# A top-k attention with a GELU layer behind it, on one core: the weights' words leave x's tile, the first loads go over three queues, and TensorE multiplies zeros until the first k

## The chip, the cores and the metric

The kernel runs on one core of a Trainium2 chip. The metric is the device time in microseconds. Before the change it is 1690.68 us (median of 3 runs, 1690.24 to 1690.7); the profiled execution spans 1690.0 us. In what follows PE is TensorE, DVE VectorE, ACT ScalarE, POOL GpSimd and SP SyncE, which here only issues DMAs.

## The reference

Attention over 8 batches, 8 heads, 576 rows and head size 64, in which each row keeps only its 32 largest scores; the heads are then joined to rows of 512, and these go through a layer of width 2048 with the exact GELU.

```
scores = scale * np.matmul(q, k.transpose(0, 1, 3, 2))
kth = np.partition(scores, -top_k, axis=-1)[..., -top_k:-top_k + 1]
scores = np.where(scores >= kth, scores, -1000000000.0)
attn = softmax(scores)                 # with 1e-9 added to the sum
attn_out = np.matmul(attn, v)
x = attn_out.transpose(0, 2, 1, 3).reshape(4608, 512)
h = x @ w_in                           # 512 x 2048
g = 0.5 * h * (1.0 + erf(h / sqrt(2)))
return g @ w_out                       # 2048 x 512
```

q, k, v and the output are float32. The two weights come as float64 numbers, so the kernel must make float32 of them itself.

## The kernel before

**Slots.** Two heads of a batch are a pair. The work is a list of items: one item is a pair and a tile of 128 rows (or, for the last 64 rows of each head, two pairs together). One turn of the main loop (line 616) is a slot, and slot n works on several items at once, in the order in which the loop writes the instructions. That order is final: each engine takes its instructions in it. In slot n, `scores(n + 2)` makes scores on PE (L291, L295) and copies them on ACT (L299, L300); `top_k(n)` finds the 32 largest of each row on DVE, with four rounds of eight maxima (L342) and three rounds that strike these out (L345); `softmax(n - 1, e)` runs on ACT (L381, L382) for the two heads; `add_small`, `threshold` and `normalise` run on POOL (L374, L357, L393); `inverse(n - 1)` is DVE's reciprocal (L368), written behind the top-k of slot n; `transposes(n - 2)` turns the attention on PE (L410 for the last columns, called the tails, then L428 for each head) and copies it on ACT (L411, L435); `attend(n - 3)` multiplies by v on PE (L459) and copies the result into xT on ACT (L464). Transposes, products by v and the small score product share two PSUM buffers ("tp").

**The layer.** Its products are cut into pieces (L507 for x times w_in, L543 for g times w_out). `mlp(1)` writes one piece, at most 7 or 8 in a slot, if the tokens that the piece needs are ready (`ready`). They become ready when all heads of a tile have been attended, in slot 10 for the first time. What is left over is written behind the last slot.

**xT.** The tile xT holds x transposed: 4 parts of 128 rows with 1152 columns, a ring over two batches.

**Weights.** The weights are cut into 16 units of 256 x 512 numbers. Unit `ORDER[i]` is finished in slot `FIRST + i`, so in slots 1 to 16. `load_weights(n + 2)`, at the end of slot n, fetches the words of a unit. The words go to a buffer that is free at that time: to rows of `w_out_sb` that have no weights yet, to an extra tile "words" of which there is one (units with i = 12 and 15), and, for i = 14 alone, to the columns from `RING - WS` = 640 on of xT, which no token needs yet. Two ACT passes make the exponents at the end of the slot before (L183, L184), a third pass makes the mantissa on ACT (L188) or, from slot `START` = 10 on, on POOL (L199), POOL adds the two (L202), and DVE puts the sign in (L210) at the end of the unit's slot.

**The start.** Ahead of the loop, lines 590 to 603 load k and q of the first two pairs, the words of the first two weight units, transpose q and k of both pairs on PE (L250, four blocks, two blocks, four blocks, each group copied by ACT or DVE in L254), and make the scores of items 0 and 1. A load of a pair is four transfers: for each head 128 KB (L94) and the last 64 rows, 16 KB, called the tail (L97). k of pair 0 goes over ACT's queue, the weights over POOL's, all else over SP's. Before its first issue POOL writes the zeros and the identity that later steps need.

**In slot 10** the loop has a case of its own (line 625): when tokens have just been attended and the next piece waits for them, the tails' transpose is written ahead of the softmaxes, so that pieces can start early.

Of the kernel before, what the change touches and what calls it, by code (L numbers as in the profile page):

```python
# [14 lines left out]
def kernel(  # L15
# [19 lines left out]
    nc = tc.nc  # L35
    f32, i32, u32 = mybir.dt.float32, mybir.dt.int32, mybir.dt.uint32
    bf16, i16, u16 = mybir.dt.bfloat16, mybir.dt.int16, mybir.dt.uint16
# [3 lines left out]
    B, H, S, D = q.shape  # L41
    P = 128
    DM = H * D
# [3 lines left out]
    NM = S // P  # L47
    SM = NM * P
    TL = S - SM
    NJ = NM + 1  # L50
    KO = DM // P
    FT = DFF // P


    RING = 2 * S
# [6 lines left out]
    ps = ctx.enter_context(tc.tile_pool(name="ps", bufs=2, space=bass.MemoryType.PSUM))  # L62
# [4 lines left out]
    w_out_sb = const.tile([P, FT, DM], f32, name="w_out_sb")  # L67
    xT = const.tile([P, KO, RING], f32, name="xT")


    raws = {n: [const.tile([P, NJ, 2, D], f32, name=f"raw_{n}{i}") for i in range(m)]
            for n, m in (("k", 2), ("q", 2), ("v", NP + 1))}
    for ts in raws.values():
        for t in ts[:2]:
            nc.gpsimd.memset(t[:, NM], 0.0)
    make_identity(nc, ident)
    for t in raws["v"][2:]:
        nc.gpsimd.memset(t[:, NM], 0.0)


# [3 lines left out]
    def raw_of(n, pair):  # L84
        return raws[n][pair % len(raws[n])]

    def load(n, pair, queue=None):
        if pair >= n_pairs:
            return
        queue = queue or nc.sync  # L90
        b, h0 = pair // NP, 2 * (pair % NP)
        t, src = raw_of(n, pair), sources[n]
        for e in range(2):
            queue.dma_start(  # L94
                out=t[:, 0:NM, e, :], in_=src[b, h0 + e, 0:SM].rearrange("(t p) d -> p t d", p=P)
            )
            queue.dma_start(out=t[e * TL : (e + 1) * TL, NM, e, :], in_=src[b, h0 + e, SM:S])  # L97

# [3 lines left out]
    WS = 512  # L104
    NWI = KO // 2 * (DFF // WS)
    UNITS = NWI + FT // 2
# [3 lines left out]
    def weights_of(u):  # L110

        if u < NWI:
            c, r = u // 2 * WS, u % 2 * 2
            return w_in, r, c, w_in_sb[:, r : r + 2, c : c + WS]
        r = 2 * (u - NWI)
        return w_out, r, 0, w_out_sb[:, r : r + 2, :]


    ORDER = [0, 1, 2, 3, 8, 9, 4, 5, 10, 11, 6, 7, 12, 13, 14, 15]
    FIRST = 1  # L120
    START = 2 * NP + 2
    words = {}
    low = const.tile([P, 1], f32, name="low")
    nc.gpsimd.memset(low, -EXP0 * 2.0**19)

    def unit_in(n):
        return ORDER[n - FIRST] if 0 <= n - FIRST < UNITS else None

    def load_weights(n, queue=None):

        queue = queue or nc.sync
        u = unit_in(n)
        if u is None:
            return
        src, r, c, dst = weights_of(u)
        if src.dtype == f32:
            for x in range(2):
                queue.dma_start(
                    out=dst[:, x], in_=src[(r + x) * P : (r + x + 1) * P, c : c + WS]
                )  # L140
            return


        half, i = src.bitcast(u16), n - FIRST
        if i != 14:
            if i not in (12, 15):
                at = FT // 2 + 4 * (i % 2)
                t = w_out_sb[:, at : at + 4, :].rearrange("p (a b) n -> p a (b n)", a=2)
            else:
                t = stage.tile([P, 2, 2 * WS], f32, tag="words", name="words")  # L150
            for a in range(2):
                queue.dma_start(
                    out=t[:, a].bitcast(u16)[:, 0 : 4 * WS - 1],
                    in_=half[(r + a) * P : (r + a + 1) * P, 4 * c + 1 : 4 * (c + WS)],
                )
        else:

            assert r + 2 < FT
            t = xT[:, :, RING - WS :]
            for a in range(2):  # L160
                queue.dma_start(
                    out=t[:, 2 * a : 2 * a + 2].bitcast(u16),
                    in_=bass.AP(
                        tensor=half.tensor, offset=half.offset + (r + a) * P * 4 * DM + 1,
                        ap=[[4 * DM, P], [2 * WS, 2], [1, 2 * WS]],
                    ),
                )
        words[u] = t

    def parts(u):  # L170

        t, dst = words[u], weights_of(u)[3]
        if t.shape[1] == 4:
            dst = dst.rearrange("p r (b n) -> p (r b) n", b=2)
        return t[:, :, 0::2], t.bitcast(u16)[:, :, 2::4], dst

    def weights_size(u):
# [11 lines left out]

    def on_pool(u):  # L190

        return ORDER.index(u) + FIRST >= START

    def weights_add(u):
        if u in words:
            w, _, dst = parts(u)
            d = dst.bitcast(i32)
            if on_pool(u):
                nc.gpsimd.tensor_scalar(  # L199
                    w.bitcast(i32), w.bitcast(u32), 2.0**-13, None, op0=ALU.mult  # L200
                )
            nc.gpsimd.tensor_tensor(d, d, w.bitcast(i32), op=ALU.add)  # L202
# [149 lines left out]
    def threshold(i):  # L352

        if i < 0 or i >= N:
            return
        st = stat_of[i]
        nc.gpsimd.tensor_scalar(  # L357
            st["neg"], st["top"][:, :, 0 :: TOPK - 1], -1.0, None, op0=ALU.mult
        )
        nc.gpsimd.tensor_tensor(  # L360
            st["bias"], st["neg"][:, :, 0], st["neg"][:, :, 1], op=ALU.subtract
        )

    def inverse(i):
        if i < 0 or i >= N:
            return
        st = stat_of[i]
        nc.vector.reciprocal(st["rden"], st["den"])  # L368

    def add_small(i):  # L370
        if i < 0 or i >= N:
            return
        st = stat_of[i]
        nc.gpsimd.tensor_scalar(st["den"], st["den"], 1e-9, None, op0=ALU.add)  # L374

    def softmax(i, e):

        if i < 0 or i >= N:
            return
        st, s = stat_of[i], row(i, e)  # L380
        nc.scalar.activation(s, s, func=AF.Prelu, bias=st["neg"][:, e, 1:2], scale=1.0, alpha=STEEP)  # L381
        nc.scalar.activation(  # L382
            s, s, func=AF.Exp, bias=st["bias"][:, e : e + 1], scale=1.0,
            accum_out=st["den"][:, e : e + 1],
        )

    def normalise(i):
        if i < 0 or i >= N:
            return
        st = stat_of[i]  # L390
        for e in range(2):
            s = row(i, e)
            nc.gpsimd.tensor_scalar(s, s, st["rden"][:, e : e + 1], None, op0=ALU.mult)  # L393
# [162 lines left out]
    pieces = []  # L556
# [18 lines left out]
    done = [0]  # L575

    def mlp(n):
        for _ in range(n):
            if done[0] >= len(pieces) or pieces[done[0]][0] > ready[0] or left[0] == 0:
                return  # L580
            pieces[done[0]][1]()
            done[0] += 1
            left[0] -= 1


    ready, left = [0], [0]
    staging = ExitStack()
    stage = staging.enter_context(tc.tile_pool(name="stage", bufs=1))

    load("k", 0, nc.scalar)  # L590
    load("q", 0)
    load("q", 1)
    load("k", 1)
    for n in range(2):
        load_weights(FIRST + n, nc.gpsimd)
    for pair in range(2):
        for piece in transpose_qk(pair, pair == 0):
            piece()
# [12 lines left out]
    for pair in range(2, n_pairs):  # L611
        b, p = divmod(pair, NP)
# [3 lines left out]
    for n in range(ahead):  # L616

        left[0] = 7 if START < n < START + 2 * NP else 8
        weights_add(unit_in(n))
        scores(n + 2)  # L620
        product = attend(n - 3)
        late = n > START + 1
        mlp(1)
        tr = transposes(n - 2)
        if product and done[0] < len(pieces) and pieces[done[0]][0] > ready[0]:

            for piece in tr[:1]:
                piece()
            tr, ready[0] = tr[1:], n_tok[0]
        softmax(n - 1, 0)  # L630
        mlp(1)
        if not late:
            softmax(n - 1, 1)
        mlp(1)
        for piece in tr[:-1]:
            piece()
            ready[0] = n_tok[0]
            mlp(1)
        ready[0] = n_tok[0]
        if late:  # L640
            softmax(n - 1, 1)
        add_small(n - 1)
        for piece in tr[-1:] + prep_in.pop(n, []):
            piece()
            mlp(1)
        mlp(left[0])
        if n < N:
            top_k(n, {3: lambda: inverse(n - 1)})
        else:
            inverse(n - 1)  # L650
        threshold(n)
        normalise(n - 1)

        weights_sign(unit_in(n))
        weights_size(unit_in(n + 1))
        if n >= FIRST:
            load_weights(n + 2)
        if n <= NP:
            load("v", n)
# [36 lines left out]
```

## Time and profile before

| | busy us of 1690.0 | instructions |
|---|---|---|
| PE | 1611.4 | 8480 |
| DVE | 1428.8 | 3042 |
| ACT | 1188.1 | 2147 |
| POOL | 662.5 | 764 |

The page has the span in 40 slices of 42 us, with the busy share of each engine in tenths, and groups of instructions by line, each with its count, busy time, mean length and the idle time ahead of it. Three places matter to this change: the first 15 us, in which the engines wait for the first loads; slot 14, from 169.5 to 189.1 us on PE; and slots 10 and 17, in which the order of the work is touched. A releaser, written behind an arrow, is what ended a wait.

### The profile page before, as it was taken

The numbers are of one execution on the slowest core, as the hardware profiler recorded it, in microseconds if no ns is written. First come the engines' busy times: TensorE is split into PE (matmuls) and PEld (weight loads), VectorE is DVE, ScalarE is ACT, GpSimd is POOL, SyncE is SP. The second block draws the span as 40 slices with busy tenths as digits, with TensorE's granted clock in tenths as the row PEclk, the third lists the DMA queues.
The fourth block names the chain that finished last, engine by engine and source line by source line (L and its number), as shares of the span: only waits on it lengthen the run. The fifth ranks groups of instructions, "written<-read, shape, count | busy, mean of one in ns | idle before, by whom it ended". The sixth has DMA issues, their size and how long they took to land.

```text
span 1690.0 us, 24403 instructions
## 1 busy us (share of the span) xinstructions
PE 1611.4 (95%) x8480; PEld 1093.3 (65%) x8480; DVE 1428.8 (85%) x3042; ACT 1188.1 (70%) x2147; POOL 662.5 (39%) x764
## 2 busy tenths in 40 slices
PE   5659899999999999999999999999999999999999
PEld 3336567676666667676666667676666666766665
DVE  6999798998889888998889888898889988899900
ACT  5778677777777777777777777777777777777730
POOL 3668743333333332333333333333333333333410
PEclk8669999999999999999999999999999999999999
DMA  6422210001100011002110111001110000000000
GB/s 158 135 91 98 78 48 9 11 18 35 29 27 15 27 29 41 1 13 49 25 31 1 35 36 41 1 14 28 32 46 1 27 15 15 21 1 13 7 13 13
DMA packets 126715, 56.10 MB, mean 33 GB/s; under 512 B 117888, under 2 KB 117888, under 8 KB 126592
## 3 DMA queue, kind: packets, MB, share of 16 engines
q1 hardware_dynamic: 125056, 52.16, 11.6%
q0 software_dynamic: 320, 2.10, 0.4%
q8 instruction: 67, 1.10, 0.3%
q14 instruction: 56, 0.46, 0.1%
q10 hardware_dynamic: 1216, 0.30, 0.1%
HBM read 45.08 MB, written 9.44 MB: 32 GB/s over the span
## 4 chain that ended last, share of the span: by engine, by line
PE 87%; ACT 5%; DVE 5%; POOL 1%; issue 1%; DMA 1%; SPq 0%; ACTq 0%; POOLq 0%
PE h_ps L507 29%; PE y_ps L543 28%; PE o L459 8%; PE s_ps L295 7%; PE tp L428 7%; DVE top L342 2%; PE o L469 2%; DVE rest L345 2%; PE tp_qk L250 2%; PE t_ps L291 2%; ACT s L382 1%; PE tp_t L410 1%; PE s_ps L316 1%; ACT s L381 1%; ACT L518 1%
## 5 line engine op out<-in xcount | busy, mean ns | idle before, releaser
L342 DVE MAX8 top<-rest 128x8 f32<-128x576 f32 x864 | 610.8, 750 | 0.0
L507 PE MATMUL h_ps<-xT,w_in_sb 128*128 128x256 f32 (+1 forms) x2560 | 554.7, 362 | 6.8 <-DMA xT<-in_moe_w_out_dram 4.9
L543 PE MATMUL y_ps<-w_out_sb,g 128*128 128x512 f32 x1152 | 549.1, 599 | 0.0
L393 POOL TENSOR_SCALAR s<-s,rden 128x576 f32<-128x576 f32 x288 | 493.5, 1723 | 0.8 <-issue 0.4
L507 PEld LDWEIGHTS h_ps<-xT,w_in_sb 128*128 128x128 f32 x2560 | 430.1, 191 | 69.4 <-issue 18.4
L345 DVE MATCH_REPLACE8 rest<-top,rest 128x576 f32<-128x576 f32 x576 | 424.3, 746 | 0.0
L374 POOL TENSOR_SCALAR den<-den 128x2 f32<-128x2 f32 x144 | 32.0, 222 | 868.7 <-ACT s L382 868.2
L543 PEld LDWEIGHTS y_ps<-w_out_sb,g 128*128 128x128 f32 x1152 | 195.4, 191 | 166.0 <-issue 164.6
L299 ACT ACTIVATE s<-s_ps 128x1024 f32<-128x1024 f32 x128 | 131.5, 1027 | 173.2 <-PE s_ps L295 153.0
L382 ACT ACTIVATE s<-s,bias 128x576 f32<-128x576 f32 x288 | 223.3, 776 | 13.2 <-ACT s L381 0.4
L381 ACT ACTIVATE s<-s,neg 128x576 f32<-128x576 f32 x288 | 223.7, 777 | 0.7 <-POOL neg L357 0.2
L435 ACT COPY pt<-tp 128x512 f32<-128x512 f32 x256 | 146.8, 575 | 98.2 <-PE tp L428 97.6
L345 DVE MATCH_REPLACE8 rest<-top,s 128x576 f32<-128x576 f32 x288 | 212.1, 746 | 0.0
L342 DVE MAX8 top<-s 128x8 f32<-128x576 f32 x288 | 202.2, 745 | 5.1 <-ACT s L300 5.1
L428 PEld LDWEIGHTS tp<-ident,s 128*128 128x128 f32 x1152 | 145.9, 144 | 93.3 <-issue 58.1
L428 PE MATMUL tp<-ident,s 128*128 128x128 f32 x1152 | 177.7, 278 | 6.4 <-ACT pt L411 6.4
L368 DVE RECIPROCAL rden<-den 128x2 f32<-128x2 f32 x144 | 23.6, 164 | 169.8 <-POOL den L374 169.5
L295 PE MATMUL s_ps<-qk 64*128 64x256 f32 x1024 | 156.5, 427 | 0.4 <-ACT s L299 0.4
L459 PE MATMUL o<-pt,raw_v 128*64 128x256 f32 x1280 | 155.1, 389 | 1.8 <-ACT pt L435 1.8
L459 PEld LDWEIGHTS o<-pt,raw_v 128*64 128x64 f32 x1280 | 87.5, 139 | 69.5 <-issue 15.1
L295 PEld LDWEIGHTS s_ps<-qk 64*128 64x128 f32 x1024 | 94.1, 198 | 24.3 <-issue 2.5
L518 ACT ACTIVATE g<-h_ps 128x512 f32<-128x512 f32 x144 | 78.7, 595 | 38.8 <-PE h_ps L507 38.0
(65 smaller groups left out, 1106.7 us busy)
## 6 DMA issues: line engine op xcount, KB each, us to landing
raw_q<-in_q_dram SPq DMA_DIRECT2D x64, 128.0 KB, 2.4
raw_v<-in_v_dram SPq DMA_DIRECT2D x64, 128.0 KB, 2.4
out_dram<-y SPq DMA_DIRECT2D x32, 256.0 KB, 2.2
raw_k<-in_k_dram SPq DMA_DIRECT2D x62, 128.0 KB, 2.4
w_out_sb<-in_moe_w_in_dram SPq DMA_DIRECT2D x12, 511.8 KB, 4.8
w_out_sb<-in_moe_w_out_dram SPq DMA_DIRECT2D x10, 511.8 KB, 3.9
w_out_sb<-in_moe_w_in_dram POOLq DMA_DIRECT2D x4, 511.8 KB, 7.7
words<-in_moe_w_out_dram SPq DMA_DIRECT2D x4, 511.8 KB, 6.5
```

The costliest lines, as they stand in the source:

```text
L295: nc.tensor.matmul(s_ps[:, e, c * 256 : (c + 1) * 256], lhsT=lhsT[rows, :], rhs=qk[rows, KT + c * 256 : KT + (c + 1) * 256], start=True, s ...
L299: nc.scalar.activation(spread(s, S + TL, SM), s_ps, func=AF.Copy, scale=scale)
L342: nc.vector.max(st["top"][:, e, 8 * r : 8 * r + 8], cur[e])
L345: nc.vector.match_replace(rest[:, e], st["top"][:, e, 8 * r : 8 * r + 8], cur[e], LOWEST)
L381: nc.scalar.activation(s, s, func=AF.Prelu, bias=st["neg"][:, e, 1:2], scale=1.0, alpha=STEEP)
L382: nc.scalar.activation(s, s, func=AF.Exp, bias=st["bias"][:, e : e + 1], scale=1.0, accum_out=st["den"][:, e : e + 1],)
L393: nc.gpsimd.tensor_scalar(s, s, st["rden"][:, e : e + 1], None, op0=ALU.mult)
L428: nc.tensor.transpose(tp[:, j * P : (j + 1) * P], s[:, first + j * P : first + (j + 1) * P], ident)
L435: nc.scalar.copy(out=dst, in_=tp.rearrange("p (j n) -> p j n", j=NM))
L459: nc.tensor.matmul(o[e * D : (e + 1) * D, 0:n], lhsT=vt[:, j, e, :], rhs=pt[:, e * NM + j if j < NM else 2 * NM, :], start=(j == 0), stop= ...
L507: nc.tensor.matmul(h_tile(u)[:, i, :], lhsT=w_in_sb[:, ko, f * P : (f + 1) * P], rhs=xT[:, ko, c0 : c0 + n], start=(ko == 0), stop=(ko == ...
L543: nc.tensor.matmul(y_of[sub], lhsT=g_of[u][:, i, sub * P : (sub + 1) * P], rhs=w_out_sb[:, f, :], start=(f == 0), stop=(f == FT - 1),)
```

## The change

Four edits. The words of unit 14 go to the one extra tile, so none are put into xT; to let that tile serve units i = 12, 14 and 15 in turn, the last unit is finished a slot later (slot 17). The first k goes over ACT's queue with its tails on POOL's, q and k of pair 1 follow on SP in the order k, q, and the words of the first two units are issued on SP behind them. PE is given 16 products of zeros, written ahead of the first transposes, for which the zeros of one v buffer are written by DVE. And the special case of the order holds only behind slot 10 (`n > START`).

```diff
-    for ts in raws.values():
-        for t in ts[:2]:
-            nc.gpsimd.memset(t[:, NM], 0.0)
+    for n, ts in raws.items():
+        for t in ts[: 1 if n == "v" else 2]:
+            (nc.vector if n == "v" else nc.gpsimd).memset(t[:, NM], 0.0)
     make_identity(nc, ident)
-    for t in raws["v"][2:]:
+    for t in raws["v"][1:]:
         nc.gpsimd.memset(t[:, NM], 0.0)
...
-    def load(n, pair, queue=None):
+    def load(n, pair, queue=None, queue2=None):
...
+        queue2 = queue2 or queue
...
-            queue.dma_start(out=t[e * TL : (e + 1) * TL, NM, e, :], in_=src[b, h0 + e, SM:S])
+            queue2.dma_start(out=t[e * TL : (e + 1) * TL, NM, e, :], in_=src[b, h0 + e, SM:S])
...
+    WARM = 16
...
-    def unit_in(n):
-        return ORDER[n - FIRST] if 0 <= n - FIRST < UNITS else None
+    SLOT_OF = {u: FIRST + i + (i == UNITS - 1) for i, u in enumerate(ORDER)}
+    UNIT_IN = {n: u for u, n in SLOT_OF.items()}
+    unit_in = UNIT_IN.get
...
-        half, i = src.bitcast(u16), n - FIRST
-        if i != 14:
-            if i not in (12, 15):
-                at = FT // 2 + 4 * (i % 2)
-                t = w_out_sb[:, at : at + 4, :].rearrange("p (a b) n -> p a (b n)", a=2)
-            else:
-                t = stage.tile([P, 2, 2 * WS], f32, tag="words", name="words")
...
-        else:
-
-            assert r + 2 < FT
-            t = xT[:, :, RING - WS :]
...
+        half, i = src.bitcast(u16), ORDER.index(u)
+        if i not in (12, 14, 15):
+            at = FT // 2 + 4 * (i % 2)
+            t = w_out_sb[:, at : at + 4, :].rearrange("p (a b) n -> p a (b n)", a=2)
+        else:
+            t = stage.tile([P, 2, 2 * WS], f32, tag="words", name="words")
...
     def on_pool(u):
 
-        return ORDER.index(u) + FIRST >= START
+        return SLOT_OF[u] >= START
...
-    load("k", 0, nc.scalar)
+    load("k", 0, nc.scalar, nc.gpsimd)
     load("q", 0)
+    load("k", 1)
     load("q", 1)
-    load("k", 1)
     for n in range(2):
-        load_weights(FIRST + n, nc.gpsimd)
+        load_weights(FIRST + n)
+
+
+    idle = raws["v"][0][:, NM].rearrange("p e d -> p (e d)")
+    warm = ps.tile([P, 512], f32, tag="l1", name="warm")
+    for _ in range(WARM):
+        nc.tensor.matmul(warm[:, 0:P], lhsT=idle, rhs=idle, start=True, stop=True)
...
-        if product and done[0] < len(pieces) and pieces[done[0]][0] > ready[0]:
+        if product and n > START and done[0] < len(pieces) and pieces[done[0]][0] > ready[0]:
```

More of the change, by code (lines that the diff above doesn't have):

```diff
@@ L141, in load_weights @@
             return
-        half, i = src.bitcast(u16), n - FIRST
-        if i != 14:
-            if i not in (12, 15):
-                at = FT // 2 + 4 * (i % 2)
-                t = w_out_sb[:, at : at + 4, :].rearrange("p (a b) n -> p a (b n)", a=2)
-            else:
-                t = stage.tile([P, 2, 2 * WS], f32, tag="words", name="words")
[L151 to L155, printed above, removed]
-        else:
-            assert r + 2 < FT
-            t = xT[:, :, RING - WS :]
[L160 to L167, printed above, removed]
+        half, i = src.bitcast(u16), ORDER.index(u)
+        if i not in (12, 14, 15):
+            at = FT // 2 + 4 * (i % 2)
+            t = w_out_sb[:, at : at + 4, :].rearrange("p (a b) n -> p a (b n)", a=2)
+        else:
+            t = stage.tile([P, 2, 2 * WS], f32, tag="words", name="words")
+        for a in range(2):
+            queue.dma_start(
+                out=t[:, a].bitcast(u16)[:, 0 : 4 * WS - 1],
+                in_=half[(r + a) * P : (r + a + 1) * P, 4 * c + 1 : 4 * (c + WS)],
+            )
         words[u] = t
@@ L172, in parts @@
         t, dst = words[u], weights_of(u)[3]
-        if t.shape[1] == 4:
-            dst = dst.rearrange("p r (b n) -> p (r b) n", b=2)
         return t[:, :, 0::2], t.bitcast(u16)[:, :, 2::4], dst
```

## The prediction

> **What bounds the kernel now.** I read the page first, then a table of busy time by stage, then the chain that ended last, then the timeline of each engine around the two places that the chain pointed to.
>
> The busy rows of the page give three regimes: a start in which no engine is full, a stretch in which VectorE (DVE) is full, and from slice 6 on a full TensorE (PE). The table by stage (columns: length, then busy us and instructions of PE, weight loads, DVE, ACT, POOL; clock; DMA share; GB/s) puts numbers on it (the first fence is the page's row of DVE in 40 slices, the second the table):
>
> ```profile
> DVE  6999798998889888998889888898889988899900
> ```
>
> ```profile
> 59.00:70.00 11.00, 5.19 (x29) 3.06 (x25) 11.00 (x23) 8.46 (x14) 7.54 (x7) 0.78 0.43 130
> ...
> 160.00:184.00 24.00, 17.38 (x87) 11.32 (x86) 19.69 (x41) 15.06 (x25) 18.00 (x11) 0.87 0.48 156
> ...
> 260.00:300.00 40.00, 40.00 (x213) 27.72 (x210) 36.34 (x79) 28.88 (x54) 14.28 (x17) 1.00 0.00 1
> ```
>
> From 15 to 135 us DVE has no gap to speak of, from about 228 us PE has next to none; what lies between is neither. So a microsecond won before 228 us is a microsecond of the end, provided nothing on the way takes it back, and one won later than that must come out of PE's own work, which the change leaves as it is.
>
> The chain shows the start. Read it as "start, length, what":
>
> ```profile
> 2.77 6.13 DMA raw_k<-in_k_dram
> ...
> 9.03 1.31 PE tp_qk L250 x5
> 10.37 0.59 ACT qk L254
> 11.01 0.80 PE t_ps L291 x2
> 11.80 2.03 PE s_ps L295 x8
> 13.86 1.02 ACT s L299
> ...
> 15.09 1.41 DVE top L342 x2
> ```
>
> The last 16 KB of the first k take 6.13 us to land; all else waits for them, and DVE begins at 15.09. In the timeline of PE, the second place:
>
> ```profile
> 173.24 0.70 PE L507 MATMUL h_ps<-xT,w_in_sb 128*128 128x256 f32 x2
> 178.84 4.63 PE L507 MATMUL h_ps<-xT,w_in_sb 128*128 128x256 f32 x10 [4.91 <-DMA xT<-in_moe_w_out_dram]
> 183.27 0.42 PE L410 MATMUL tp_t<-ident,s 128*128 128x128 f32 x1
> ```
>
> PE sits for 4.91 us until the words of a weight unit, put into xT by L161, have landed, although these products read xT's columns 0 to 255 and the words lie from column 640 on. ACT waits 4.54 us for the same transfer. Then PE runs slow: ten products in 4.63 us, where twelve of the same shape take 2.86 us at 137 us.
>
> **What the Trainium skill says.** *TensorE: Matmul & The Clock Gate*, Part 1 (the HAM clock gate): PE starts at half clock and gets the full one only after a busy window of about 3.4 us; the window runs freely. The trace agrees and is stricter: after 178.84 the full pace comes only near 184.6, 5.8 us later, that is after one whole window without a gap. At the start PE is still at half pace at 24.4 us. *DMA: Bandwidth & Descriptors*, Queues, rings and completion order: each DMA engine takes turns between the queues, a packet at a time. The trace agrees: between 6 and 8 us the queue with the 4 KB packets of weights had 86.0% of the share and the SP queue with its 256-byte packets 4.6%. Same page, Anatomy of one DMA (the gpsimd path): about 2.0 us fixed for a DMA that GpSimd issues; the trace has its first such packets about 1.4 us after the issue at 2.84.
>
> **The change, part by part.**
>
> *1. First loads.* k's big transfers keep ACT's queue, its tails go to POOL's, the weights go behind q and k on SP. 576 KB of k0 and q0 at the 220 GB/s of 2 to 4 us, from 1.9 us, end at 4.5. k's two big transfers were issued at 0.73 and 1.87 and will be issued at 0.73 and 1.3; they then land near 4.7 (before: 5.2). The tails are issued by POOL after its memsets, which ended at 2.88 and are one shorter, so at 2.7 and 3.3; with 1.4 us to the first packet and about 1 us to finish, the last lands at 5.7; with the page's 2.0 us flat it is 5.3, with the 3.2 us of the quickest weight transfer 6.5. q0's tail (6.9 before, with weights in its way) lands near 5.5. So data are there at 5.7, 3.2 us sooner than 8.9. k1 and q1 are no longer behind weights either. The weights' words land about 15 us; ACT first reads them at the end of slot 0 (24.97 before, about 22 after): hidden.
>
> *2. Products of zeros.* The page has 256 instructions for the 128 t_ps products, so a full product is two instructions, and 16 are 32. Warm, twenty of this shape (L469) take 2.50 us: (2.50-0.27)/19 = 0.117 us each. Cold is not shown in a row long enough: 0.22 from the transposes, up to 0.37 from a pair of t_ps at 11.01 (0.80 less 0.42). I take twice the warm one, 0.235. They start when DVE's memset is done, about 1.1 us. If the clock is released between 4.5 and 7.9 (the first whole window of 3.4 us), they end between 6.6 and 8.3; I take 7.7. So **PE, not the data (5.7), sets the start**: it is in order, and the transposes of k stand behind the zeros. From there all is warm: four transposes of k 0.44; then the chain quoted above, 6.06 us from 9.03 to 15.09, less 0.65 on five transposes, 0.4 on t_ps, 1.0 on s_ps: 4.0. DVE begins at 7.7+0.44+4.0 = 12.1, a gain of **3.0** (2.4 to 4.2; with the slow cold end and a late release, 9.5+4.4 = 13.9, it is 1.2). Without the products it would be 5.9+6.06 = 12.0: they bring next to nothing. DVE is full from then to slot 10, so the whole gain travels.
>
> *3. No words in xT.* In slot 14 (169.5 to 189.1 on PE) I walk the order written in the loop without the wait. ACT: copy of o at 173.3, softmax to 175.3; PE: 12 products to 175.9, tails 176.1, transposes and products to 181.2; ACT's second softmax ends at 179.7 instead of 187.7; DVE, which ends its top-k at 180.1, gets its reciprocal at 180.2 instead of 188.06. PE's next slot begins at 181.2 instead of 189.12. The gain is **7.9**: 4.9 wait, 2.4 slow clock after it, and 0.6 of ACT's copies. The lower end is 7.3, PE's part alone. The words now need the one stage buffer of unit 12; its last reader, DVE's sign of slot 13, is done at 170.6, and SP issues at 173.4 anyway, behind the four loads of q and k. They land by 178 to 180 (4.5 to 6.5 us) and ACT asks for them at 181.5. No new wait, with 1.5 us to spare; SP's next work is a slot later.
>
> *4. Slot 10 in another order.* With `n > START` the tails' copy on ACT stands behind both softmaxes (3.1 us), as in slots up to 9, where the trace shows the price:
>
> ```profile
> 118.89 1.12 PE L428 MATMUL tp<-ident,s 128*128 128x128 f32 x4 [1.88 <-ACT pt L411]
> ...
> 224.16 2.38 PE L459 MATMUL o<-pt,raw_v 128*64 128x256 f32 x20 [1.77 <-ACT pt L435]
> ```
>
> There are two PSUM buffers for these transposes, so the third needs that copy. In slot 10 ACT's softmaxes end at 130.9, the copy at 131.2; PE, which did that group at 130.47 after one more piece of products, would come to it at 129.6 and wait 1.6. The last product then ends 1.5 later, ACT's second gelu (which already waited 0.97 for it) too, and in slots 11 to 13 DVE waits for ACT in each (0.81, 1.97, 0.52), so nothing swallows it: **-1.5** (0 to -1.7).
>
> *5. Unit 15 a slot later.* ACT's two passes (2.3 us) leave slot 16's start, where ACT then waits for PE's o anyway, and enter slot 17's, where ACT had 0.9 us free. The second line above is the place: PE waits there for ACT's copy at 224.1, which comes about 1.25 later. **-1.2** (0 to -1.4). POOL's 5.4 us and DVE's 1.35 move into a slot with room. The memset of raw_v on DVE is hidden, DVE is idle.
>
> The sum: 3.0+7.9-1.5-1.2 = 8.2 us; 1690.7-8.2 = **1682.5**.
>
> **The rivals.** (B) *Parts 4 and 5 are swallowed* by waits on other engines: for it, ACT's order in slot 10 starts the softmax 0.15 earlier; against it, ACT is the releaser in all these waits. 3.0+7.9 = 10.9: 1679.8. (C) *The zeros eat the start*: cold to the end at 0.25 each, PE is free at 9.1 and still slow: 9.1+0.87+6.06 = 16.0, nothing won or 0.9 lost. 7.9-2.7-0.5 = 4.7: 1686.0. For it: 13 us of ragged work did not warm PE before; against: that work had gaps, the zeros have none. (D) *A transfer takes the wait's place*: the words of unit 14 come late behind the loads of q and k and ACT's queue stands instead of PE: 3.0+0-2.7 = 0.3: 1690.4. Against: the 1.5 us of slack. (E) *Slower*: C and D together, 0-0.5-2.7 = -3.2, at worst with 1.6 us more for a colder PE: 1694 to 1695.5.
>
> **Chances.** My forecast 0.60, B 0.18, C 0.14, D 0.05, E 0.03. The range takes in B and C with their spread: 1678 to 1687. Faster by over 0.2% (below 1687.3): 0.60+0.18+0.14 and a little of D's spread: 0.92; the same: 0.05; slower: 0.03.
>
> **What would show it.** The first DVE maximum at about 12.1; 32 more PE instructions, ending near 7.7, the first transpose right behind them; no wait for a DMA in PE's list; slot 14 about 11.5 us instead of 19.6; in slot 10 a PE wait of about 1.6 us for ACT's copy, in slot 17 one of about 3 us. I am wrong if the words' landing or SP's queue appears as a releaser of ACT, if DVE is no longer full from 12 to 130, or if PE past 228 us shows gaps that it did not have.

## The result, and the profile after

The changed kernel takes **1685.08 us** (median of 6 runs, 1683.64 to 1688.61), the kernel before beside it 1690.69 (6 runs, 1689.13 to 1691.72): a ratio of 0.997 with a 95% interval from 0.9957 to 0.9983. It is faster by 5.6 us; the forecast was 1682.5 in a range from 1678 to 1687. The profiled execution of it spans 1682.0 us, that of before 1690.0; the device times of these two are 1683.78 and 1691.79, so they lie 8.0 us apart where the medians lie 5.6 apart. One execution of e3 below took 3166.05 us at a clock of 0.89, where the others had 0.98, and counts in no number here.

The rows of the page for the span in 40 slices, PE of the kernel before, then PE and DVE of the changed kernel:

```profile
PE   5659899999999999999999999999999999999999
...
PE   5559999999999999999999999999999999999999
...
DVE  7998988998889888998989888898889998899900
```

The regimes are the old ones, DVE full first and then PE, but the 8 in slice 5, where PE stood for the words, is gone: PE shows a 9 from slice 4 on. The table by stage (length, then busy us and instructions of PE, weight loads, DVE, ACT, POOL; clock; DMA share; GB/s):

```profile
59.00:70.00 11.00, 3.40 (x19) 2.45 (x20) 11.00 (x25) 10.34 (x19) 7.53 (x7) 0.65 0.48 142
160.00:184.00 24.00, 22.26 (x127) 13.20 (x126) 23.48 (x48) 20.85 (x36) 21.93 (x16) 1.00 0.27 84
260.00:300.00 40.00, 40.00 (x205) 27.99 (x204) 34.82 (x77) 29.58 (x53) 16.21 (x20) 1.00 0.01 1
```

In the second window PE is busy for 22.26 us, where it was for 17.38, and its clock is full. The first and the third window show what did not move: DVE full at 59 to 70, PE full at 260 to 300. (PE's clock is lower in the first, 0.65 instead of 0.78; the ledger below has nothing lost there, since DVE is full.) The chain that ended last, at its start ("start, length, what"):

```profile
1.04 5.40 PE warm L590 x32
6.44 0.45 PE tp_qk L239 x4
...
9.48 1.09 PE s_ps L284 x8
10.59 1.02 ACT s L288
...
11.81 1.41 DVE top L331 x2
```

The products of zeros end at 6.4, the score products run at the full pace (1.09 us for eight, 2.03 before), and DVE begins at 11.81 instead of 15.09. No transfer stands in this chain: PE itself, not the data, sets the start. (The packets of weights that were in the way before are of 8 KB, 256 of 8188 bytes in the trace of before, not of 4 KB as the prediction has it; this changes nothing in its argument.) Slot 14 in the timeline of PE:

```profile
171.23 2.86 PE L496 MATMUL h_ps<-xT,w_in_sb 128*128 128x256 f32 x12
173.93 0.27 PE L399 MATMUL tp_t<-ident,s 128*128 128x128 f32 x1
174.03 1.02 PE L532 MATMUL y_ps<-w_out_sb,g 128*128 128x512 f32 x2
```

Twelve products in 2.86 us without a gap, where before two were followed by 4.91 us of waiting and ten slow ones. The waits of PE from 95 us to the end (line, whom it waited for; us in total, times, longest):

```profile
PE tp_t L399 <- POOL s L382: 11.2, 4, 6.0
PE tp L417 <- ACT pt L400: 3.8, 2, 2.3
...
PE o L448 <- ACT pt L424: 1.8, 1, 1.8
...
PE t_ps L280 <- ACT pt L424: 1.4, 2, 1.2
...
PE tp_t L404 <- POOL s L382: 0.4, 1, 0.4
```

No line of this list names a DMA. What is left are waits for ACT and POOL.

**A ledger by slots.** DVE's reciprocal closes each slot, so its start in two traces tells how much has been won up to there. For slots 10, 12, 14, 16 and 19 it starts at 132.72, 157.59, 188.06, 212.19 and 246.43 us before the change. The gains of the profiled executions against these, in us (the column "start" is the first maximum of DVE against 15.09):

| kernel | start | slot 10 | slot 12 | slot 14 | slot 16 | slot 19 | span |
|---|---|---|---|---|---|---|---|
| after | 3.28 | 3.35 | 2.04 | 9.94 | 10.12 | 7.77 | 8.0 |
| e12, the same again | 2.94 | 3.00 | 1.72 | 9.63 | 9.81 | 7.46 | 7.7 |
| e1, old order of slot 10 | 2.69 | 2.76 | 1.48 | 9.44 | 9.53 | 5.62 | 5.8 |
| e2, no zeros | 2.10 | 2.11 | 2.51 | 10.44 | 10.59 | 6.54 | 6.7 |
| e3, words alone | 1.03 | 1.10 | 0.93 | 8.88 | 9.02 | 5.26 | 4.3 |
| e4, start alone | 2.71 | 2.68 | 1.37 | 1.20 | 1.28 | 1.28 | 1.3 |
| e5, filled waits | 2.15 | 2.26 | 2.32 | 10.27 | 10.43 | 8.09 | 8.3 |
| e6, last unit in slot 18 | 2.08 | 2.12 | 0.52 | 8.48 | 8.62 | 8.61 | 8.8 |
| e7, e6 filled | 2.17 | 2.22 | 2.34 | 10.31 | 10.37 | 10.37 | 10.6 |
| e8, e7 with 8 zeros | 4.00 | 4.03 | 4.42 | 12.36 | 12.52 | 12.52 | 12.7 |
| e10, the same as e8 | 3.30 | 3.34 | 3.73 | 11.67 | 11.83 | 11.81 | 12.0 |
| e9, e7 without zeros | 2.10 | 2.21 | 1.07 | 9.04 | 9.15 | 9.15 | 9.4 |
| e11, before, filled | 1.46 | 1.44 | 1.87 | 2.31 | 2.39 | 2.38 | 2.4 |

Each row is one execution, and so is the row of zeros that they are taken against. That one had a late start: e3 and e11 load and begin as the kernel before does, and their DVE starts at 14.06 and 13.63. Differences along a row hardly depend on this; the column "start" does. The traced executions lie up to 1.7 us off the medians of their kernels (that of e11 1.7 under it, those of e4 and before 1.3 and 1.1 over it), so the ledger tells where time goes, and the medians how much of it there is.

Along the row of after: the words bring 9.94 - 2.04 = 7.90 us; 3.35 - 2.04 = 1.31 are lost between slots 10 and 12, and 10.12 - 7.77 = 2.35 between slots 16 and 19. The experiments ask where these two losses come from, and what the zeros are worth.

### The profile page after: what moved, and what is told of

The parts are those of the page before. It is cut to its first block, busy times and chain, and to the rows that moved or that the text cites. A ratio compares the mean times of both kernels' runs of the same rounds, so it can differ in the third digit from the quotient of the medians.

```text
span 1682.0 us, 24466 instructions
## 1 busy us (share of the span) xinstructions
PE 1608.8 (96%) x8512; PEld 1095.1 (65%) x8512; DVE 1428.6 (85%) x3043; ACT 1189.3 (71%) x2147; POOL 661.9 (39%) x761
## 3 DMA queue, kind: packets, MB, share of 16 engines
HBM read 45.08 MB, written 9.44 MB: 32 GB/s over the span
## 4 chain that ended last, share of the span: by engine, by line
PE 88%; DVE 6%; ACT 4%; issue 1%; POOL 1%; ACTq 0%; POOLq 0%
PE h_ps L496 30%; PE y_ps L532 28%; PE o L448 8%; PE s_ps L284 7%; PE tp L417 7%; DVE top L331 3%; DVE rest L334 3%; PE o L458 2%; PE tp_qk L239 2%; PE t_ps L280 2%; PE tp_t L399 1%; PE s_ps L305 1%; ACT s L371 1%; ACT L507 1%; ACT s L370 1%
## 5 line engine op out<-in xcount | busy, mean ns | idle before, releaser
L284 PE MATMUL s_ps<-qk 64*128 64x256 f32 x1024 | 152.6, 418 | 0.7 <-ACT s L288 0.7
```

The costliest lines, as they stand in the source:

```text
L284: nc.tensor.matmul(s_ps[:, e, c * 256 : (c + 1) * 256], lhsT=lhsT[rows, :], rhs=qk[rows, KT + c * 256 : KT + (c + 1) * 256], start=True, s ...
```

## The experiments

In e1 to e4 the first theory is that of the prediction (the copy on ACT in slot 10 and the two passes of the last unit on ACT take back 1.5 and 1.2 us, the zeros bring next to nothing); the others, and those of the later runs, are named in the expectations. Edits are against the changed kernel, except in e11. e1 to e4 shared one series of the kernel before (median 1690.54), e5 to e8 one (1690.14), e9 to e11 one (1691.01); e12 has its own (1691.06). The ratios are against these.

**e1: slot 10 in the old order.**

```diff
-        if product and n > START and done[0] < len(pieces) and pieces[done[0]][0] > ready[0]:
+        if product and done[0] < len(pieces) and pieces[done[0]][0] > ready[0]:
```

> The changed kernel with the old order in slot 10 put back (the tails' transpose ahead of the softmaxes). Theory on record: the new order costs 1.5 us in slot 10, so this runs 1.5 us below the changed kernel (near 1683.5 against its 1685.1). Rival, from the trace of the changed kernel: PE stands at the tails' transpose for POOL in slot 10 whatever the order, the order costs nothing, and the 1.7 us that were lost between slots 11 and 12 are TensorE's half clock after a wait of 2.3 us; then this runs within 1 us of the changed kernel.

1685.03 us (8 runs), ratio 0.9968 (0.9958 to 0.9979): the time of the changed kernel. From slot 9's reciprocal to slot 11's it takes 22.50 us, the changed kernel 22.56. So the order of slot 10 costs nothing. The tails' transpose in the timeline of PE, first of the changed kernel, then of e1:

```profile
123.54 0.33 PE L399 MATMUL tp_t<-ident,s 128*128 128x128 f32 x1 [1.88 <-POOL s L382]
123.71 1.03 PE L496 MATMUL h_ps<-xT,w_in_sb 128*128 128x256 f32 x4
```

```profile
124.11 0.33 PE L399 MATMUL tp_t<-ident,s 128*128 128x128 f32 x1 [0.62 <-POOL s L382]
124.28 1.89 PE L496 MATMUL h_ps<-xT,w_in_sb 128*128 128x256 f32 x8
```

In either order this transpose waits for POOL's normalised scores, which the prediction did not see (before the change it stood at 127.27 without a wait). When it is through, at 123.5, ACT's softmaxes are nearly done (125.1), the copy follows at 125.22, and the third group, at 125.88, finds its buffer free. The loss between slots 10 and 12 is the same in e1 (2.76 - 1.48 = 1.28), so it is not the order's.

**e2: no products of zeros.**

```diff
-    WARM = 16
+    WARM = 0
```

> The changed kernel without the 16 products of zeros. Theory on record: the data are there at about 5.7 us and the rest of the start runs at half clock, DVE's first maximum comes at 12.0 instead of 11.8, and the time is that of the changed kernel within 0.5 us. Rival: the zeros carry the gain of the start; without them DVE begins at 14 us or later and the time is 2 us or more above the changed kernel.

1685.06 us (5 runs), ratio 0.9966 (0.9954 to 0.9979): no difference in the median. DVE starts at 12.99 instead of the 12.0 worked out; PE at the start:

```profile
5.25 1.09 PE L239 MATMUL tp_qk<-ident,raw_k 128*128 128x128 f32 x4 [5.25 <-DMA raw_k<-in_k_dram]
...
7.12 1.12 PE L239 MATMUL tp_qk<-ident,raw_q 128*128 128x128 f32 x4 [0.36 <-DVE qk L243]
...
9.64 2.08 PE L284 MATMUL s_ps<-qk 64*128 64x256 f32 x8
```

The large blocks of k are there at 5.25 (4.7 was forecast; the tails, forecast at 5.7, have landed when they are needed at 6.34), and all of it then runs at half pace. In this trace nothing is lost between slots 10 and 12 (2.11, 2.51), which is new, but 4.05 us between slots 16 and 19, 1.7 more than in the changed kernel. So the equal medians don't show that the zeros do nothing: in the traces a later start and a larger loss stand against a loss that is absent.

**e3: the words alone.** The start and the order of slot 10 are those of before, there are no zeros; the words of unit 14 in their tile and the last unit a slot later stay.

```diff
...
-    WARM = 16
+    WARM = 0
...
-    load("k", 0, nc.scalar, nc.gpsimd)
+    load("k", 0, nc.scalar)
...
-        load_weights(FIRST + n)
...
+        load_weights(FIRST + n, nc.gpsimd)
...
-        if product and n > START and done[0] < len(pieces) and pieces[done[0]][0] > ready[0]:
+        if product and done[0] < len(pieces) and pieces[done[0]][0] > ready[0]:
```

> The kernel before with one part alone: the words of unit 14 in the extra tile and the last unit in slot 17; start and order of slot 10 as before. Theory: slot 14 shrinks by 7.9 us, slot 17 gives back 1.2: 6.7 us below the kernel before (1684.0). Rival: the words' wait was hidden by DVE or ACT and a wait of another kind takes its place: less than 3 us.

1687.91 us (19 runs), ratio 0.9984 (0.9978 to 0.9991). Slot 14 brings 8.88 - 0.93 = 7.95 us, as forecast, and slots 16 to 19 take 9.02 - 5.26 = 3.76 back, three times the forecast. About 1 us more is lost at the very end: PE's last product ends 5.31 us sooner than before the change (1680.89 against 1686.20), but from there to the end of the span, in which ACT's last copy and the last transfers of the output remain, it takes 4.8 us instead of 3.8.

**e4: the start alone.** The start with its zeros stays; words and order are those of before.

```diff
-    SLOT_OF = {u: FIRST + i + (i == UNITS - 1) for i, u in enumerate(ORDER)}
+    def unit_in(n):
+        return ORDER[n - FIRST] if 0 <= n - FIRST < UNITS else None
...
+            t = xT[:, :, RING - WS :]
...
-        if product and n > START and done[0] < len(pieces) and pieces[done[0]][0] > ready[0]:
+        if product and done[0] < len(pieces) and pieces[done[0]][0] > ready[0]:
```

> The kernel before with the other part alone: first loads over three queues, weights behind them, zeros on PE; the words still go into xT and the order of slot 10 is the old one. Theory: DVE begins 3.3 us sooner and all of it reaches the end: 1687.4. Rival: the gain of the start is swallowed by the free-running clock window further on (slots 9 to 18): anything from 0 to 5 us with a spread between runs of 2 us or more, where the kernel before spreads over 1 to 2.6 us.

1689.99 us (13 runs), ratio 0.9996 (0.9988 to 1.0004): a gain that can't be told from none. The trace has 2.7 us at the start and 1.37 at slot 12: half of it is gone before the words' wait, which is still there (5.5 us). With the words and the order untouched, the loss between slots 10 and 12 belongs to the start.

**The half clock.** The place of that loss, the last transposes of slot 11 and what follows them on PE, in the changed kernel and then in the kernel before:

```profile
140.73 1.02 PE L417 MATMUL tp<-ident,s 128*128 128x128 f32 x4 [2.29 <-ACT pt L400]
141.55 1.92 PE L496 MATMUL h_ps<-xT,w_in_sb 128*128 128x256 f32 x4
143.25 1.06 PE L239 MATMUL tp_qk<-ident,raw_k 128*128 128x128 f32 x4
```

```profile
144.44 0.66 PE L428 MATMUL tp<-ident,s 128*128 128x128 f32 x4 [2.26 <-ACT pt L411]
144.93 1.03 PE L507 MATMUL h_ps<-xT,w_in_sb 128*128 128x256 f32 x4
145.80 0.60 PE L250 MATMUL tp_qk<-ident,raw_k 128*128 128x128 f32 x4
```

Both wait 2.3 us for ACT, but behind the wait the changed kernel runs the same instructions at about half pace until 144 us, and DVE's wait in slot 12 grows from 1.97 to 3.66 us. The profile has the granted clock, the share of its full speed that PE is given: from 142 to 144 us it is 0.50 in the changed kernel, and 1.00 from 140 to 148 in the kernel before. So the new theory was that PE's clock falls in this wait. It can be tried by filling the wait.

**e5: products of the identity in the waits.** Nine ahead of the last transposes of slot 11, two ahead of the scores and seven behind them in slot 18; their results are not used.

```diff
+    def fill(t, count):
+        for _ in range(count):
+            nc.tensor.matmul(t, lhsT=ident, rhs=ident, start=True, stop=True)
...
+        if n == 18:
...
+            fill(h_tile(8)[:, 0, 0:P], 2)
         scores(n + 2)
+        if n == 18:
+            fill(h_tile(8)[:, 0, 0:P], 7)
...
+        if n == 11:
+            fill(ps.tile([P, 512], f32, tag="l2", name="fill")[:, 0:P], 9)
```

> The changed kernel with further products (identity times identity, into PSUM that is overwritten or not in use, their result is not used) where PE waits: 9 ahead of the last transposes of slot 11, 2 ahead of the scores and 7 ahead of the product by v of slot 18. Theory: these waits themselves are short, but two of them within one clock window halve PE's clock for the next 3.4 us and so cost 1.7 us each; with PE busy there the clock stays: 1.7 us less in slot 18 in nearly every execution and 1.7 us less in slot 11 or 12 in about half of them, 1682.5 in the median, and a smaller spread. Rival: the half clock there is hidden by ACT and POOL; then the added 4 us of products only delay PE and the time stays at 1685 or rises to 1687.

1683.46 us (5 runs, 1682.39 to 1683.91), ratio 0.9959 (0.9945 to 0.9972); its interval overlaps that of the changed kernel, so the trace has to decide. The place in e5's timeline of PE:

```profile
139.68 2.17 PE L614 MATMUL fill<-ident 128*128 128x128 f32 x18
142.12 0.66 PE L417 MATMUL tp<-ident,s 128*128 128x128 f32 x4 [0.27 <-ACT pt L400]
142.61 1.03 PE L496 MATMUL h_ps<-xT,w_in_sb 128*128 128x256 f32 x4
```

ACT's copy comes no sooner, yet all behind it is at full pace, and nothing is lost up to slot 12 (2.26, 2.32). That settles where the first loss comes from: work that is thrown away wins it back (in the median e7 shows it). The second is as large as before, 2.34, so it does not come from the clock here.

**e6: the last unit in slot 18.**

```diff
-    SLOT_OF = {u: FIRST + i + (i == UNITS - 1) for i, u in enumerate(ORDER)}
+    SLOT_OF = {u: FIRST + i + 2 * (i == UNITS - 1) for i, u in enumerate(ORDER)}
```

> The changed kernel with the last unit one slot later still (slot 18), so that ACT's two passes for it fall at the end of slot 17, where ACT then waits 3.1 us for PE. Theory: these passes stand in slot 17 between PE and its transposes and bring the wait of 1.2 us, a longer wait for POOL and the half clock behind them, 2.4 to 4.0 us together; all of it is won back: 1681.5 in the median. Rival: only ACT's own delay of 1.2 us is won: 1683.9.

1683.22 us (5 runs, 1682.57 to 1683.47), ratio 0.9958 (0.9945 to 0.997). Between slots 16 and 19 nothing is lost any more (8.62, 8.61). Two things went. First, in the timeline of PE, the changed kernel and then e6:

```profile
212.17 0.49 PE L280 MATMUL t_ps<-qk 128*128 128x128 f32 x2 [1.22 <-ACT pt L424]
...
215.49 4.07 PE L448 MATMUL o<-pt,raw_v 128*64 128x256 f32 x20 [1.77 <-ACT pt L424]
```

```profile
212.29 0.43 PE L280 MATMUL t_ps<-qk 128*128 128x128 f32 x2
...
215.54 2.38 PE L448 MATMUL o<-pt,raw_v 128*64 128x256 f32 x20 [1.77 <-ACT pt L424]
```

The wait of 1.22 us for ACT is gone (1.46 us in the reciprocal of slot 17: 223.97 - 215.31 = 8.66, against 10.12 a slot before). ACT's two passes now stand here, where it had nothing to do:

```profile
215.39 1.16 ACT L172 ACTIVATE size<-words 128x1024 bf16<-128x1024 bf16 x1
216.59 1.15 ACT L173 ACTIVATE w_out_sb<-size,low 128x1024 int32<-128x1024 int16 x1
```

Second, POOL. In the changed kernel DVE puts the sign into the last unit right behind slot 17's reciprocal, and just then POOL is to make the bias of the next softmax. DVE, then POOL, of the changed kernel, and POOL of e6:

```profile
215.40 1.35 DVE L199 SCALAR_TENSOR_TENSOR w_out_sb<-words,w_out_sb 128x1024 uint16<-128x1024 uint16 x1
```

```profile
215.67 1.09 POOL L349 TENSOR_TENSOR bias<-neg 128x2 f32<-128x2 f32 x1
216.75 3.42 POOL L382 TENSOR_SCALAR s<-s,rden 128x576 f32<-128x576 f32 x2
```

```profile
215.73 0.19 POOL L349 TENSOR_TENSOR bias<-neg 128x2 f32<-128x2 f32 x1
215.90 3.43 POOL L382 TENSOR_SCALAR s<-s,rden 128x576 f32<-128x576 f32 x2
```

POOL's small instruction takes 1.09 us instead of 0.19 and ends with DVE's pass (215.40 + 1.35 = 216.75). The Trainium skill, *SBUF — State Buffer*, SBUF: two separate sides, says that DVE and POOL share a pair of ports under an exclusive lock, which a DVE operation with two SBUF inputs takes; the trace agrees to 0.01 us. The normalised scores come 0.85 us later (they are begun at 216.75 instead of 215.90), and PE's transposes of slot 18 wait for them. That is the rest: of the 2.35 us of the ledger 1.46 are lost up to slot 17's reciprocal and 0.89 behind it. That e6 wins both back is measured; which part is ACT's and which POOL's is read off the traces, since e6 moves both at once. The unit that stood a slot earlier before had the same 1.09 at 212.55, where nobody waited for it.

**e7: e6 with the fill of slot 11, and seven products in slot 18.**

```diff
-    SLOT_OF = {u: FIRST + i + (i == UNITS - 1) for i, u in enumerate(ORDER)}
+    SLOT_OF = {u: FIRST + i + 2 * (i == UNITS - 1) for i, u in enumerate(ORDER)}
...
         scores(n + 2)
+        if n == 18:
...
+            fill(h_tile(8)[:, 0, 0:P], 7)
...
+        if n == 11:
+            fill(ps.tile([P, 512], f32, tag="l2", name="fill")[:, 0:P], 9)
```

> Both: the last unit in slot 18, 9 products of the identity in slot 11 and 7 ahead of the product by v of slot 18 (their result is not used). Theory: 0.85 us less than e6 in the median (half of the executions lose 1.7 us in slot 12), 1680.7, with a spread under 2 us. Rival: the spread comes from elsewhere and stays at 4 us.

1681.2 us (5 runs, 1680.07 to 1681.66), ratio 0.9946 (0.9934 to 0.9959). The two repairs add up: 2.22, 2.34, 10.31, 10.37 and 10.37 along the row. Against e6, in the same series, the median falls by 2.0 us and the ranges don't touch; between slots 16 and 19 the ledger has nothing lost in either, so this is the fill of slot 11. With it the start's gain does travel to the end.

**e8: e7 with 8 products of zeros.**

```diff
-    WARM = 16
+    WARM = 8
```

> As e7 with 8 products of zeros at the start instead of 16. Theory: the data are there at 5.25 us while the 16 products hold PE until 6.3 to 6.9; 8 end by 4.6 to 5.0, DVE begins 1 us sooner if the clock was freed by then (about 10.9) and at 13 if not: between 1 us less and 0.6 us more than e7. Rival: DVE's begin doesn't reach the end at all and the two are alike within 0.3 us.

1679.05 us (5 runs, 1678.95 to 1680.55), ratio 0.9937 (0.9925 to 0.995). **e10** is the same kernel again.

> e8 a second time, with another start of the clock's window. Theory: DVE begins between 10.5 and 12.0 depending on where the window stands, 1679 to 1680.5. Rival: e8 had luck, and this runs at 1681.

1679.49 us (5 runs, 1678.79 to 1681.38), ratio 0.9934 (0.992 to 0.9948). DVE starts at 11.09 in e8 and 11.79 in e10. PE at the start of e7 and of e8:

```profile
1.04 6.50 PE L590 MATMUL warm<-raw_v 128*128 128x128 f32 x32 [1.04 <-DVE raw_v L75]
7.38 0.60 PE L239 MATMUL tp_qk<-ident,raw_k 128*128 128x128 f32 x4
```

```profile
1.04 3.78 PE L590 MATMUL warm<-raw_v 128*128 128x128 f32 x16 [1.04 <-DVE raw_v L75]
5.41 0.75 PE L239 MATMUL tp_qk<-ident,raw_k 128*128 128x128 f32 x4 [0.58 <-DMA raw_k<-in_k_dram]
```

Eight products end at 4.8, before the data; sixteen hold PE for 2 us after these have landed. And in e8 eight do as much for the clock: the transposes behind them are nearly as quick. In e10 they do not: there the clock, granted at 4.75, falls again at 8.17, and the eight score products take 2.08 us, as in the kernel before. Even so it starts sooner than the mean of sixteen, 12.52.

**e9: e7 without zeros.**

```diff
-    WARM = 16
+    WARM = 0
```

> As e7 without any products of zeros at the start. Theory: 16 products bring nothing, since they hold PE past the data, and 8 bring about 1.9 us, since they end just before the data and the clock is freed sooner: this runs like e7 (1681.2 within 0.5 us) and DVE begins at 13.0. Rival: the zeros are worth nothing at all and the 2.1 us between e7 and e8 were chance: this runs like e8, 1679.

1682.25 us (5 runs, 1680.78 to 1683.33), ratio 0.9949 (0.9936 to 0.9961). Its start is that of e7 (12.99 and 12.92), so zeros would bring nothing; but 2.21 - 1.07 = 1.14 us are lost in slot 11. PE in slot 10:

```profile
124.73 0.48 PE L399 MATMUL tp_t<-ident,s 128*128 128x128 f32 x1 [3.86 <-POOL s L382]
125.00 1.91 PE L496 MATMUL h_ps<-xT,w_in_sb 128*128 128x256 f32 x4
126.71 1.06 PE L417 MATMUL tp<-ident,s 128*128 128x128 f32 x4
```

Behind 3.86 us of waiting PE is at half pace here too; the fill covers slot 11 alone. Taken together, zeros against none in this arrangement: eight 2 to 3 us (1682.25 less 1679.05 and 1679.49; the ratios have 0.9949 less 0.9937 and 0.9934). Sixteen (1681.2, ratio 0.9946) can't be told from none.

**e11: the kernel before with the fill of slot 11.**

```diff
+        if n == 11:
+            fill(ps.tile([P, 512], f32, tag="l2", name="fill")[:, 0:P], 9)
```

> The kernel before with 9 products of the identity (not used further) ahead of the last transposes of slot 11. Theory: the wait of 2.26 us there halves the clock in a part of the executions of the kernel before too; filled, the median falls by about 0.8 us and the slow end of its spread by 1.7 us. Rival: only the changed kernel has that loss (the new start or the new order brings it): no change within 0.3 us.

1691.11 us (13 runs), ratio 0.9999 (0.9991 to 1.0007): nothing that can be told from none. The interval rules out a gain of more than 1.5 us, but not the 0.8 of the theory. So the fill is no good in itself. Of the kernels without a fill, all five with zeros (after, e12, e1, e4, e6) lost 1.3 to 1.6 us in slot 12, and none of the three without (before, e2, e3). Why work at 1 us should decide on a clock at 140 us is taken up behind e12.

**e12: the changed kernel again.**

> The changed kernel once more. Theory: its spread of some 5 us comes from where the clock's free-running window stands; in this execution slots 17 and 18 lose 2 to 4 us against the kernel before again, since the waits there come to 3 us or more in every one, while the start (DVE's first maximum anywhere between 11.8 and 13.0) and slot 12 (1.7 us lost or not) differ from execution to execution; the median is 1684 to 1686. Rival: start and slots 11 to 18 are alike to 0.3 us in every execution of one kernel, and the spread lies behind slot 19.

1684.16 us (5 runs, 1683.78 to 1687.2), ratio 0.9964 (0.995 to 0.9977). The row of the ledger repeats: 1.28 lost up to slot 12 and 2.35 between 16 and 19, though in slot 18 its products by v are at full pace (2.38 us, not 4.07). They then wait longer for POOL, 0.68 and 1.40 us; in the changed kernel's trace slow products hid that wait. So a slow clock there costs nothing so long as POOL ends last. In e1, e2 and e3 it came after POOL's wait, on eight layer products (3.38 to 3.46 us for 1.89), and there it cost the 1.4 to 1.7 by which their losses exceed 2.35.

**Where the windows lie.** In each of the fourteen traces all changes of the granted clock lie on a grid of 3.41 us, and in each execution the grid stands elsewhere against the start. Cut along it, the time around slot 11's wait reads as follows, first in the changed kernel, then in the kernel before (length, PE's busy us first; the clock is third from the end):

```profile
137.47:140.88 3.41, 1.12 (x7) 0.67 (x6) 2.94 (x8) 3.37 (x8) 2.75 (x3) 1.00 0.68 276
140.88:144.29 3.41, 3.41 (x13) 2.95 (x13) 3.41 (x8) 0.87 (x2) 3.29 (x4) 0.50 0.02 5
```

```profile
140.25:143.66 3.41, 1.93 (x11) 1.34 (x10) 3.41 (x8) 3.29 (x6) 2.77 (x2) 1.00 1.00 406
143.66:147.07 3.41, 2.63 (x16) 2.40 (x17) 2.60 (x5) 2.43 (x7) 2.58 (x4) 1.00 0.20 79
```

In the changed kernel the wait (138.44 to 140.73) lies in one window. PE works for 1.12 us of it, and for the whole next window it is given half the clock. In the kernel before, a border cuts a wait of the same length (142.18 to 144.44), and the clock stays. The other traces without a fill agree: with 1.11 to 1.17 us of work in the window the clock fell (after, e12, e1, e4, e6); with 1.54 and then 3.04 (e2), or 1.79 and 2.79 (e3), it did not, and with the fill (e5, e7, e8, e10), which leaves 3.1 us or more, it did not either. So the same wait is cheap or dear by where it falls on the grid.

The zeros tie the kernel to the grid. They run slow up to the border at which the clock is granted, and DVE's first maximum follows that border: in order of time the borders are 4.34, 5.04, 5.52, 5.57, 6.67, 6.69 and 6.83 us (after, e12, e4, e1, e7, e5, e6), and the maxima come in the same order, from 11.81 to 13.01. In the five with zeros and no fill, slot 11's wait then begins 0.01 to 0.29 of a window behind a border, so that all of it fits into one; in before, e2 and e3 it begins 0.45 to 0.57 behind one. That it fell so in these five follows from this tie, as far as the traces tell; that it never did without zeros rests on three executions and may be chance. Nor is there a sharp threshold: with 1.65 us of work in a window of slot 18 the clock fell in the changed kernel (212.55 to 215.97) and stayed in e12 (213.26 to 216.67).

## Why the prediction was right or wrong, step by step

**The direction and the words (7.9): right.** 7.90 and 7.95 measured. As forecast, no wait took its place: the words, issued at 172.31, are read by ACT at 179.47 without a wait, and PE's list has no DMA.

**The start (3.0, DVE at 12.1): right in the profile, too large as a mean.** The trace has 3.28. But "DVE begins at 15.09" was taken as fixed, and it was one execution. Over three traces with the old start it begins at 15.09, 14.06 and 13.63, mean 14.26; over seven with the new start and 16 zeros at 11.81, 12.15, 12.40, 12.38, 12.94, 13.01 and 12.92, mean 12.52. That is 1.7 us. "PE, not the data, sets the start" held (k's large blocks at 5.25, PE free at 6.4 to 7.5). That zeros "bring next to nothing" held for sixteen (12.99 without them); the 12.0 without them was 1 us too low: k's first four transposes, at half pace, keep PE until 6.3, and not 5.9, and q's transposes then wait for DVE's copy out of a PSUM buffer (until 7.12, 0.8 us behind k's tails, where it was 0.24 before). What I did not ask was whether fewer would do: eight are better.

**"DVE is full from then to slot 10, so the whole gain travels": failed** behind slot 10. 1.3 us are lost in slot 12.

**Slot 10 in another order (-1.5): failed.** It costs nothing (e1). The PE wait of 1.6 us did not come, because PE already stands for POOL at the tails. A loss of nearly this size is there, a slot later and for another reason: PE's clock halves in a wait of 2.3 us that lies in one window (e5 and e7 remove it). I had counted that wait only as time, as it was before.

**Unit 15 a slot later (-1.2): right in mechanism, too small.** The PE wait of "about 3 us" is there, as two (1.22 + 1.77 = 2.99; the second was there before), and 1.46 us are lost up to slot 17's reciprocal, where ACT's passes stand. Missing was DVE's sign, "a slot with room": it blocks POOL's bias for 0.9 us, and PE's transposes stand behind that. 2.35 in all (e6).

**The sum.** With the measured terms 1.7 + 7.9 - 1.3 - 2.35 = 5.95 us; the medians have 5.6 and, in the second series, 6.9. The forecast of 8.2 was high by the start's mean (1.3) and the last unit (1.15); the wrong reason in slot 10 had nearly the right size by luck.

**The rivals.** B needs parts 4 and 5 hidden: part 4 was, part 5 was not. C, zeros that keep PE slow, did not come (1.09 us for the score products), but its idea is right in part: sixteen hold PE for longer than the data need. D and E did not come: the words had landed when ACT asked.

## What to carry to other kernels

A wait of PE has two prices, its length and, when too much of it falls into one window of the clock, the slow work behind it. Where PE waits anyway, products of anything can save the second, and a run with them tells whether there is one. A change at the start can move all that follows against the windows. Work that is moved to an engine's free time must be placed in front of a wait of that engine, and every engine that takes part in it must be looked at, also for what shares a port with it. Size warm-up work to end when the data land, and take the start of a kernel from several executions before it is a base for a gain.

## What the runs showed of the hardware that was not expected

- The Trainium skill, *TensorE: Matmul & The Clock Gate*, Part 1, gives an idle window of about 3.4 us for the fall to half clock. Here PE was slow behind waits of 2.25 to 2.31 us (after, e1, e4, e6, e12) and, in other executions, at full pace behind 2.25 and 2.26 (e2, e3, before). The measurement decides: a window need not be idle for the fall, 1.1 us of work in 3.41 did not prevent it, and the length of a wait alone doesn't tell.
- The same 32 instructions of zeros took 5.40 to 6.58 us in seven executions, depending on when the clock was granted (at 4.34 and at 6.83 us in these two).
- A POOL instruction of 0.19 us on 128x2 numbers took 1.09 us beside a DVE pass, and ended with it to 0.01 us.
- The same first loads brought DVE to its first maximum between 13.63 and 15.09 us (before, e3, e11).

**Open:** how much work in a window keeps the clock; whether the kernel before also loses it in slot 11 in some executions; the rest of the changed kernel's spread (5 us over its runs, 1.5 in e5); why e3's last transfers took 1 us longer. Not tried: the last unit in its old slot with the words out of xT, since units 14 and 15 would then need the one words tile in two slots that follow each other. The best kernel measured is e8, 0.63% below the kernel before (0.9937, 0.9925 to 0.995), and 0.9934 in its repetition e10.
